# Two subtractions on the next pair's x, ordered behind a unit's last product on VectorE

## The chip, the cores and the metric

One Trainium2 chip, one core of it. The metric is the device time of one execution in microseconds (us); lower is better. The time before is the median of three runs.

## What is computed

Attention for 8 batches of 8 heads (576 positions, head size 64, a mask by blocks of 64), then a bilinear layer on its output: two products with 512 x 1536 weights, multiplied element by element, and a third product back to 512. In the reference:

```python
scores = scale * np.matmul(q, k.transpose(0, 1, 3, 2))
scores = np.where(mask, scores, -1000000000.0)
attn = np.exp(scores - np.max(scores, axis=-1, keepdims=True))
attn = attn / (np.sum(attn, axis=-1, keepdims=True) + 1e-09)
x = (attn @ v).transpose(0, 2, 1, 3).reshape(B * S, H * D)   # 4608 x 512
a, b = x @ w_a, x @ w_b                                      # 4608 x 1536 each
return (a * b) @ w_out                                       # 4608 x 512
```

## The kernel before

The kernel works with float32 values split in a high part that TensorE multiplies exactly (`fp32r`) and a low part, the remainder; a product is then three matmuls, high by high, high by low and low by high. ScalarE makes the high part with a cast (L110, L662 to L666), VectorE or GpSimd the low part with a subtraction (L113, L669 to L673).

Up to about 720 us attention and the first four of twelve blocks of the hidden size run together. The rest is the stage of the change: two passes (`ps_` 0 and 1) over six pairs (`tt` 0 to 5) of 384-column halves of x. A pair is worked on in **four units** (`pair_unit`, hidden blocks f = 4 to 7 in the first pass, 8 to 11 in the second) and then in **`pair_out`**, 96 matmuls into eight output tiles `pso`. In names such as `u_z_2_7` the first number is the pair and the second the block; the fourth unit of a pair has f = 7 or 11.

A unit forms seven products instead of eight (a Strassen-like scheme, which is why sums of x and of weights are needed). TensorE makes four products y, x, w, v; then three more are added on top of x, w and v in PSUM, each of which must wait until VectorE has read the sum that stands there: L708 (`u = x + u`) comes before the second product into x, L710 before that into w, L712 before that into v. L714 to L718 give the two results of the unit; the last, L718, is recorded as `last["hf"]`. ScalarE (L110) and GpSimd (L113) split each result in `h` tiles, high and low, which `pair_out` reads. `pair_out` starts with the first two output tiles over three units (18 matmuls) and then needs the `h` tiles of the fourth unit with index 1, high and low.

For the next pair `sums_x` makes the seven sums of x, once for each half of the 512 channels (`kp` 0 and 1). For each half it has four subtractions on VectorE (L659, L660, L661, L664; the first two need only the loaded x), four casts on ScalarE into `xh` (L662, L663 and L666 need the subtractions, L665 needs only the loaded x), and the remainders `xl`: for `kp` 0 all on VectorE, for `kp` 1 the first two on VectorE (L669, L670) and two on GpSimd (L672, L673). `xh` has three buffers and `xl` two, so a cast for `kp` 1 waits until TensorE has read the present pair's `xh` of `kp` 0 for the last time, near the end of the fourth unit. The loaded x, `xr`, has four buffers; a load waits until the remainders of the pair before are done. Loads and stores of this stage go through SyncE's queue in order.

`sums_x` is called in two steps: for `kp` 0 after the third unit (i = 2), for `kp` 1 after the fourth. The calls only write the instructions down. Where they end up on each engine is decided by a scheduler, which orders them by its own estimates and by dependences. `behind_of(ins, "hf")` adds an order without a semaphore: `ins` stands on its engine behind the instruction recorded last under that key. In the first pass up to pair 4 VectorE also converts weights for the second pass in the background (L139 to L178); these steps are already paced with `behind_of`.

Every engine runs its instructions in the order in which they stand.

Of the kernel before, what the change touches and what calls it, by code (L numbers as in the profile page):

```python
# [14 lines left out]
ALU = mybir.AluOpType  # L15
# [37 lines left out]
def attention_then_bilinear_ffn(  # L53
# [51 lines left out]
    def f32(ap):  # L105
        return ap.bitcast(F32)
# [10 lines left out]
    def behind_of(ins, key):  # L117
        if key in last:
            tc.add_manual_dep(ins.ins, last[key].ins.name, NOSYNC, reason="after work that is waited for")
# [533 lines left out]
    def sums_x(raw, kp, nm):  # L653

        hi = xk.tile([P, NW, T2], F32R, tag="xh", name=f"xh_{nm}_{kp}", bufs=3)
        t = tpool.tile([P, 3, T2], F32, tag="xt", name=f"xt_{nm}_{kp}")
        a, b = raw[2 * kp:2 * kp + 2]
        v = nc.vector
        v.tensor_tensor(t[:, 1], b[:, 1], a[:, 1], op=ALU.subtract)  # L659
        v.tensor_tensor(a[:, 1], a[:, 1], a[:, 0], op=ALU.subtract)  # L660
        v.tensor_tensor(t[:, 0], b[:, 1], a[:, 1], op=ALU.subtract)  # L661
        nc.scalar.copy(hi[:, 0:2], a)  # L662
        nc.scalar.copy(hi[:, 2:4], t[:, :2])  # L663
        v.tensor_tensor(t[:, 2], b[:, 0], t[:, 0], op=ALU.subtract)  # L664
        nc.scalar.copy(hi[:, 4:6], b)  # L665
        nc.scalar.copy(hi[:, 6], t[:, 2])  # L666
        yield
        lo = xk.tile([P, NW, T2], F32R, tag="xl", name=f"xl_{nm}_{kp}", bufs=2)
        v.tensor_tensor(lo[:, 0:2], a, f32(hi[:, 0:2]), op=ALU.subtract)  # L669
        v.tensor_tensor(lo[:, 2:4], t[:, :2], f32(hi[:, 2:4]), op=ALU.subtract)  # L670
        e = nc.gpsimd if kp else v
        e.tensor_tensor(lo[:, 4:6], b, f32(hi[:, 4:6]), op=ALU.subtract)  # L672
        e.tensor_tensor(lo[:, 6], t[:, 2], f32(hi[:, 6]), op=ALU.subtract)  # L673
        yield hi, lo
# [96 lines left out]
    for kp in range(KP):  # L771
        g = sums_x(raw, kp, "0_0")
        next(g)
        xs.append(next(g))
# [7 lines left out]
    for ps_ in range(2):  # L782
        fs = list(range(F1 + ps_ * F2, F1 + (ps_ + 1) * F2))
        for tt in range(NT2):
# [18 lines left out]
            nm = f"z{ps_}_{tt}"  # L803
            for i, f in enumerate(fs):
                if ps_ == 0 and tt == 0:
                    background(PER_F * (i + 1))
                for _ in pair_unit(f, xs, f"{nm}_{f}", hs, i == 0):
                    k += 1
                    background(start + k * T2 / 2.4 / pace)
                if i == 0 and not lastp:  # L810
                    raw = load_x((tt + 1) % NT2)
                if i == 1:
                    for x in todo[:6]:
                        load_part(*x)
                if i == 2 and not lastp:
                    nxt = [sums_x(raw, kp, f"{ps_}_{tt + 1}") for kp in range(KP)]
                    next(nxt[0])
                if ps_ == 0 and tt == NT2 - 1:
                    new_w(f + F2)
                    for kp in range(KP):  # L820
                        nc.sync.dma_start(
                            f32(w_sb[f + F2][0][:, kp]).rearrange("p j c n -> p (j c n)"), wabd[f - F1, kp])
# [53 lines left out]
```

## Time and profile before

| what | value |
| --- | --- |
| median of 3 runs (lowest, highest) | 1304.1 us (1302.88, 1304.73) |
| the profiled execution: its time, its span | 1307.22 us, 1305.4 us |
| TensorE busy | 1254.8 us, 96% of the span |
| VectorE, ScalarE, GpSimd busy | 997.9, 679.3, 546.4 us |
| mean granted TensorE clock | 0.984 |

In the profile PE is TensorE, PEld its weight loads, DVE VectorE, ACT ScalarE, POOL GpSimd and SP SyncE. Busy time is the union of an engine's instructions; "idle before" is the engine's pause ahead of an instruction, with what ended it. The profiled execution took 3.1 us more than the median of the plain runs.

### The profile page before, as it was taken

How to read it: one execution, taken by the hardware profiler on the slowest of the kernel's cores; microseconds unless marked ns; L12 is line 12 of the kernel's file. 1: busy time of each engine (PE TensorE's matmuls, PEld its weight loads, DVE VectorE, ACT ScalarE, POOL GpSimd, SP SyncE). 2: the span in 40 equal slices, each digit the busy share in tenths (PEclk: the TensorE clock that was granted, in tenths of full speed). 3: DMA queues.
4: the chain of work that ended last, by engine and by line, in shares of the span. 5: the costliest groups of instructions: out<-in, count | busy, mean ns of one | idle time of the engine just before them, and what ended most of it. 6: DMA issues, size and time to landing. Idle time of an engine off the chain costs nothing.

```text
span 1305.4 us, 23282 instructions
## 1 busy us (share of the span) xinstructions
PE 1254.8 (96%) x7849; PEld 1179.0 (90%) x7849; DVE 997.9 (76%) x2325; ACT 679.3 (52%) x1722; POOL 546.4 (42%) x681
## 2 busy tenths in 40 slices
PE   9998999999999999999998998999999899999998
PEld 5678888989999899898998998998999899999998
DVE  6878777777777777777789999899986476577563
ACT  5787777777777777777745433233332122222210
POOL 4676565555555555545521323124123124123131
PEclk8999999999999999999998999999999899999999
DMA  5557756667667676676234353563556541342231
GB/s 192 147 152 209 190 145 174 175 165 176 162 161 185 155 178 159 153 176 163 62 122 140 126 191 126 169 212 126 196 164 247 186 137 55 101 145 79 68 97 61
DMA packets 93495, 196.57 MB, mean 151 GB/s; under 512 B 11968, under 2 KB 52928, under 8 KB 93376
## 3 DMA queue, kind: packets, MB, share of 16 engines
q1 hardware_dynamic: 88768, 185.64, 50.3%
q10 hardware_dynamic: 4608, 9.44, 1.9%
q8 instruction: 63, 1.03, 0.3%
q14 instruction: 56, 0.46, 0.1%
HBM read 96.47 MB, written 47.19 MB: 110 GB/s over the span
## 4 chain that ended last, share of the span: by engine, by line
PE 58%; DVE 16%; DMA 11%; ACT 7%; issue 4%; SPq 1%; POOL 1%; ACTq 0%; DVEq 0%; POOLq 0%
PE pso_z L736 14%; PE ps L217 7%; PE psx_z L690 6%; PE psw_z L690 6%; PE psv_z L690 6%; PE tp L463 4%; DMA kp<-kT 4%; DMA k<-kp 4%; PE s L394 4%; PE psy_z L690 3%; PE av L507 2%; PE pso L217 2%; DMA q<-qp 2%; ACT ah L465 2%; DVE al L467 2%
## 5 line engine op out<-in xcount | busy, mean ns | idle before, releaser
L113 POOL TENSOR_TENSOR h_z<-u_z,h_z 128x384 fp32r<-128x384 f32 x96 | 113.6, 1184 | 399.3 <-ACT h_z L110 386.5
L217 PE MATMUL ps<-xh,wab 128*128 128x288 f32 x1024 | 240.6, 302 | 2.4 <-ACT a L241 2.4
L736 PE MATMUL pso_z<-h_z,wo 128*128 128x384 f32 x1152 | 207.1, 339 | 5.3 <-POOL h_z L113 5.3
L736 PEld LDWEIGHTS pso_z<-h_z,wo 128*128 128x128 f32 x1152 | 202.6, 190 | 7.8 <-POOL h_z L113 7.7
L467 DVE TENSOR_TENSOR al<-tp,ah 128x512 fp32r<-128x512 f32 x224 | 137.9, 617 | 65.0 <-ACT ah L465 61.6
L217 PEld LDWEIGHTS ps<-xh,wab 128*128 128x128 f32 x1024 | 172.6, 189 | 6.6 <-ACT a L241 2.7
L442 POOL TENSOR_SCALAR e<-e,rc 128x512 f32<-128x512 f32 (+3 forms) x256 | 153.2, 610 | 44.0 <-DVE rc L439 37.1
L217 PE MATMUL ps<-xl,wab 128*128 128x288 f32 x512 | 155.7, 304 | 0.0
L463 PE MATMUL tp<-ident,e 128*128 128x128 f32 x832 | 135.3, 277 | 10.6 <-DVE s L415 4.6
L465 ACT CAST ah<-tp 128x512 fp32r<-128x512 f32 x224 | 119.4, 535 | 44.6 <-PE tp L463 44.5
L110 ACT CAST h_z<-u_z 128x384 fp32r<-128x384 f32 x96 | 49.4, 514 | 165.0 <-DVE u_z L715 160.4
L690 PE MATMUL psx_z<-xh,wab 128*128 128x384 f32 x384 | 118.5, 344 | 7.7 <-DVE u_z L708 7.3
L217 PE MATMUL pso<-hh,wo 128*128 128x288 f32 x512 | 120.5, 305 | 3.2 <-ACT hh L110 3.1
L463 PEld LDWEIGHTS tp<-ident,e 128*128 128x128 f32 x832 | 102.3, 142 | 22.3 <-issue 6.2
L690 PE MATMUL psw_z<-xh,wab 128*128 128x384 f32 x384 | 117.0, 341 | 0.9 <-DVE u_z L710 0.8
L690 PE MATMUL psv_z<-xh,wab 128*128 128x384 f32 x384 | 117.0, 340 | 0.5 <-DVE u_z L712 0.4
L400 DVE TENSOR_REDUCE nm<-s 128x1 f32<-128x192 f32 (+3 forms) x256 | 109.5, 430 | 2.9
L403 ACT ACTIVATE e<-s,nm 128x192 f32<-128x192 f32 (+2 forms) x192 | 101.6, 529 | 7.1 <-DVE nm L400 4.4
L113 POOL TENSOR_TENSOR v<-vr,v 128x320 fp32r<-128x320 f32 x56 | 49.9, 891 | 127.2 <-ACT v L110 98.0
L217 PEld LDWEIGHTS ps<-xl,wab 128*128 128x128 f32 x512 | 96.5, 188 | 3.8
L113 POOL TENSOR_TENSOR hl<-hf,hh 128x288 fp32r<-128x288 f32 x64 | 54.1, 845 | 103.1 <-ACT hh L110 99.2
L217 PEld LDWEIGHTS pso<-hh,wo 128*128 128x128 f32 x512 | 88.3, 194 | 5.2 <-ACT hh L110 3.9
(147 smaller groups left out, 3013.7 us busy)
## 6 DMA issues: line engine op xcount, KB each, us to landing
k<-kp SPq DMA_DIRECT2D x112, 288.0 KB, 4.0
xr<-xd SPq DMA_DIRECT2D x48, 384.0 KB, 3.5
pt<-part SPq DMA_DIRECT2D x96, 192.0 KB, 3.5
q<-qp SPq DMA_DIRECT2D x112, 160.0 KB, 2.7
raww<-wab SPq DMA_DIRECT2D x24, 512.0 KB, 3.9
qp<-qT SPq DMA_DIRECT2D x32, 320.0 KB, 3.1
vr<-vm SPq DMA_DIRECT2D x64, 160.0 KB, 3.1
kp<-kT SPq DMA_DIRECT2D x32, 288.0 KB, 3.5
```

What stands on the lines that cost most here:

```text
L110: nc.scalar.copy(hi, src)
L113: return lo_eng.tensor_tensor(lo, src, f32(hi), op=ALU.subtract)
L217: mm = nc.tensor.matmul(ps, w_, d_, start=(i == 0), stop=(i == n - 1))
L394: mark = nc.tensor.matmul(ps[:, :w], qm[:, q0[t]:q0[t] + P], kk[:, :w], start=(i == 0), stop=(i == len(ks) - 1))
L400: nc.vector.tensor_reduce(nm[:, t:t + 1], view, axis=AX.X, op=ALU.max, negate=True)
L403: nc.scalar.activation(out, view, AF.Exp, bias=bias, accum_out=sm[:, t, :1])
L442: nc.gpsimd.tensor_scalar(ev, ev, rc[:, t:t + 1], 1.0, op0=ALU.mult, op1=ALU.mult)
L463: mark = nc.tensor.transpose(tp[:, c], src, ident)
L465: nc.scalar.copy(ah[:, :m, cols], tp[:, :m])
L467: nc.vector.tensor_tensor(al[:, :m, cols], tp[:, :m], f32(ah[:, :m, cols]), op=ALU.subtract)
L690: nc.tensor.matmul(ps, wt[:, i, iw], j[:, ix], start=start and kp == 0 and i == 0 and j is xh, stop=kp == KP - 1 and i == 1, skip_group_ch ...
L736: nc.tensor.matmul(ps, wt[:, a, osl], b, start=i == 0, stop=i == 3 * len(fs) - 1)
```

## The change

The first two subtractions of `sums_x`, for both halves `kp`, get `behind_of(..., "hf")`, except for the very first pair (`0_0`). When `kp` 0 is written down, the last recorded product is that of the third unit; when `kp` 1 is, it is already that of the fourth.

```diff
         v = nc.vector
-        v.tensor_tensor(t[:, 1], b[:, 1], a[:, 1], op=ALU.subtract)
-        v.tensor_tensor(a[:, 1], a[:, 1], a[:, 0], op=ALU.subtract)
+        for ins in (v.tensor_tensor(t[:, 1], b[:, 1], a[:, 1], op=ALU.subtract),
+                    v.tensor_tensor(a[:, 1], a[:, 1], a[:, 0], op=ALU.subtract)):
+            if nm != "0_0":
+                behind_of(ins, "hf")
         v.tensor_tensor(t[:, 0], b[:, 1], a[:, 1], op=ALU.subtract)
```

The scheduler then places more than these two differently. From L661 on, lines have two more in their number after the change (L665 becomes L667, L672 becomes L674, L708 becomes L710, L736 becomes L738). In the lists below a row is one instruction: line, operation, written and read tiles, shape.

VectorE across the end of pair 5 of the first pass and the start of the second pass, before. `xt_1` and `xr_1` belong to the pair after the next one; `pt` rows add an output tile:

```order
L673 TENSOR_TENSOR xl_6_0_13253<-xt_6_0_13173,xh_6_0_13172 128x384
L669 TENSOR_TENSOR xl_6_1_13268<-xr_0_13020,xh_6_1_13258 128x768
L670 TENSOR_TENSOR xl_6_1_13268<-xt_6_1_13259,xh_6_1_13258 128x768
L795 TENSOR_TENSOR pt_0_5_0_13092<-pso_0_z_5_13273,pt_0_5_0_13092 128x384
L795 TENSOR_TENSOR pt_1_5_0_13094<-pso_1_z_5_13283,pt_1_5_0_13094 128x384
L795 TENSOR_TENSOR pt_2_5_0_13096<-pso_2_z_5_13307,pt_2_5_0_13096 128x384
L795 TENSOR_TENSOR pt_3_5_0_13098<-pso_3_z_5_13322,pt_3_5_0_13098 128x384
L795 TENSOR_TENSOR pt_0_5_0_13100<-pso_0_z_5_13337,pt_0_5_0_13100 128x384
L659 TENSOR_TENSOR xt_1_0_13621<-xr_1_13472,xr_1_13470 128x384
L660 TENSOR_TENSOR xr_1_13470<-xr_1_13470 128x384
```

and after the change:

```order
L675 TENSOR_TENSOR xl_6_0_13253<-xt_6_0_13173,xh_6_0_13172 128x384
L659 TENSOR_TENSOR xt_6_1_13259<-xr_0_13022,xr_0_13020 128x384
L797 TENSOR_TENSOR pt_0_5_0_13092<-pso_0_z_5_13273,pt_0_5_0_13092 128x384
L660 TENSOR_TENSOR xr_0_13020<-xr_0_13020 128x384
L797 TENSOR_TENSOR pt_1_5_0_13094<-pso_1_z_5_13283,pt_1_5_0_13094 128x384
L663 TENSOR_TENSOR xt_6_1_13259<-xr_0_13022,xr_0_13020 128x384
L671 TENSOR_TENSOR xl_6_1_13268<-xr_0_13020,xh_6_1_13258 128x768
L666 TENSOR_TENSOR xt_6_1_13259<-xr_0_13022,xt_6_1_13259 128x384
L672 TENSOR_TENSOR xl_6_1_13268<-xt_6_1_13259,xh_6_1_13258 128x768
L797 TENSOR_TENSOR pt_2_5_0_13096<-pso_2_z_5_13307,pt_2_5_0_13096 128x384
```

The subtractions for the pair after the next one have left this place; the next pair's `kp` 1 has moved into it. The same holds at the ends of the other pairs.

ScalarE at the end of the same pair, before (the `h_z_5_7_1` row is the cast that `pair_out` needs first):

```order
L110 CAST h_z_5_6_0_13135<-u_z_5_6_13139 128x384
L662 CAST xh_6_1_13258<-xr_0_13020 128x768
L663 CAST xh_6_1_13258<-xt_6_1_13259 128x768
L110 CAST h_z_5_7_1_13215<-u_z_5_7_13218 128x384
L665 CAST xh_6_1_13258<-xr_0_13022 128x768
```

and after:

```order
L110 CAST h_z_5_6_0_13135<-u_z_5_6_13139 128x384
L664 CAST xh_6_0_13172<-xr_0_13016 128x768
L665 CAST xh_6_0_13172<-xt_6_0_13173 128x768
L668 CAST xh_6_0_13172<-xt_6_0_13173 128x384
L667 CAST xh_6_1_13258<-xr_0_13022 128x768
L110 CAST h_z_5_7_1_13215<-u_z_5_7_13218 128x384
```

The cast of `xr` that GpSimd's remainder reads (L665, now L667) has become the first cast for `kp` 1 and stands ahead of the `h` cast.

GpSimd at the same place, before:

```order
L113 TENSOR_TENSOR h_z_5_6_0_13136<-u_z_5_6_13139,h_z_5_6_0_13135 128x384
L113 TENSOR_TENSOR h_z_5_7_1_13216<-u_z_5_7_13218,h_z_5_7_1_13215 128x384
L672 TENSOR_TENSOR xl_6_1_13268<-xr_0_13022,xh_6_1_13258 128x768
L673 TENSOR_TENSOR xl_6_1_13268<-xt_6_1_13259,xh_6_1_13258 128x384
L113 TENSOR_TENSOR h_z_5_7_0_13214<-u_z_5_7_13217,h_z_5_7_0_13213 128x384
```

and after:

```order
L113 TENSOR_TENSOR h_z_5_6_0_13136<-u_z_5_6_13139,h_z_5_6_0_13135 128x384
L674 TENSOR_TENSOR xl_6_1_13268<-xr_0_13022,xh_6_1_13258 128x768
L113 TENSOR_TENSOR h_z_5_7_1_13216<-u_z_5_7_13218,h_z_5_7_1_13215 128x384
L113 TENSOR_TENSOR h_z_5_7_0_13214<-u_z_5_7_13217,h_z_5_7_0_13213 128x384
L675 TENSOR_TENSOR xl_6_1_13268<-xt_6_1_13259,xh_6_1_13258 128x384
```

The remainder of 768 columns has moved ahead of the low part that `pair_out` needs first. This swap is new at the ends of pairs 2 to 5 of the first pass and 0 to 4 of the second; at the ends of pairs 0 and 1 of the first pass GpSimd has this order already before the change.

On TensorE the order changes only in the first pass, among the units of pair 0 and near the ends of pairs 0 to 4. At pairs 1 to 4, six or seven of `pair_out`'s first 18 matmuls move ahead of the fourth unit's last products (ahead of the second product into x: 3, 2, 4 and 6 of them); at pair 0, five that stood there move back behind the unit.

## The prediction

> **What bounds the kernel now.** I read the page's busy times first, then the busy times by stretch, then TensorE's waits in the stage of the pairs, then the single pauses in the timeline.
>
> ```profile
> PE 1254.8 (96%) x7849; PEld 1179.0 (90%) x7849; DVE 997.9 (76%) x2325; ACT 679.3 (52%) x1722; POOL 546.4 (42%) x681
> 850.00:900.00 50.00, 48.96 (x275) 47.16 (x275) 47.86 (x85) 17.36 (x31) 14.56 (x12) 1.00 0.53 177
> 1100.00:1150.00 50.00, 50.00 (x286) 49.67 (x285) 34.86 (x56) 13.90 (x25) 15.65 (x12) 1.00 0.34 103
> PE psx_z L690 <- DVE u_z L708: 7.3, 9, 3.9
> PE pso_z L736 <- POOL h_z L113: 5.3, 3, 2.5
> ```
>
> TensorE is the bound: 50.00 of 50 us in a stretch of the second pass, 48.96 in the first pass, where VectorE with 47.86 is nearly full. So only what makes TensorE pause counts, and there are two such things (total us, times, longest): the sum x + u from VectorE (L708), and the low part `h` from GpSimd (L113) at a pair's end. The larger pauses one by one:
>
> ```profile
> 757.13 1.32 PE L736 MATMUL pso_z<-h_z,wo 128*128 128x384 f32 x5 [2.44 <-POOL h_z L113]
> 799.97 0.44 PE L690 MATMUL psx_z<-xh,wab 128*128 128x384 f32 x1 [0.51 <-DVE u_z L708]
> 809.28 1.01 PE L736 MATMUL pso_z<-h_z,wo 128*128 128x384 f32 x2 [2.54 <-POOL h_z L113]
> 852.78 0.44 PE L690 MATMUL psx_z<-xh,wab 128*128 128x384 f32 x1 [0.35 <-DVE u_z L708]
> 901.66 0.45 PE L690 MATMUL psx_z<-xh,wab 128*128 128x384 f32 x1 [0.95 <-DVE u_z L708]
> 949.51 0.44 PE L690 MATMUL psx_z<-xh,wab 128*128 128x384 f32 x1 [0.28 <-DVE u_z L708]
> 956.61 1.68 PE L736 MATMUL pso_z<-h_z,wo 128*128 128x384 f32 x8 [0.36 <-POOL h_z L113]
> 1024.85 0.69 PE L690 MATMUL psx_z<-xh,wab 128*128 128x384 f32 x1 [3.89 <-DVE u_z L708]
> ```
>
> The L736 rows are the ends of pairs 0, 1 and 4 of the first pass; the first four L690 rows are the fourth units of pairs 1 to 4; the last is the first unit of the second pass. A pause also costs clock afterwards. In stretches of 3.4 us (the number after the ACT and POOL columns is the granted clock):
>
> ```profile
> 140.10:143.50 3.40, 1.89 (x11) 1.42 (x11) 3.24 (x12) 3.24 (x9) 2.55 (x4) 1.00 0.66 185
> 143.50:146.90 3.40, 2.41 (x17) 2.16 (x17) 2.82 (x9) 1.92 (x7) 3.40 (x5) 1.00 0.30 62
> 689.70:693.10 3.40, 1.61 (x10) 1.40 (x11) 3.33 (x6) 1.38 (x4) 0.91 (x1) 1.00 0.00 1
> 693.10:696.50 3.40, 3.40 (x16) 3.40 (x16) 3.06 (x8) 1.79 (x5) 1.14 (x1) 0.50 0.58 192
> 757.90:761.30 3.40, 3.40 (x13) 3.40 (x12) 3.40 (x4) 1.35 (x2) 1.59 (x2) 0.50 0.67 199
> 809.10:812.50 3.40, 3.22 (x10) 3.22 (x11) 3.40 (x3) 0.83 (x1) 3.11 (x3) 0.50 0.65 222
> 1024.20:1031.00 6.80, 6.15 (x19) 6.15 (x20) 2.83 (x6) 0.51 (x1) 0.07 (x1) 0.50 0.89 340
> ```
>
> A stretch with TensorE idle for 1.8 us (busy 1.61) is followed by half clock; one idle for 1.5 us (busy 1.89) is not. Half clock costs half of the busy time in it: 1.7 us after pair 0, 1.6 after pair 1, 3.1 after the pass boundary. By the Trainium skill (TensorE: Matmul & The Clock Gate, "Part 1: The HAM clock gate") the clock is halved after at least one idle window of about 3.4 us. The rows above disagree: 1.8 us were enough. Were the Trainium skill right to the letter, none of the 2 us pauses that I forecast below would cost clock, and the time would be that of the third rival.
>
> **The change part by part.** First, **the pass boundary**. The subtractions for the pair after the next one leave VectorE's queue here:
>
> ```profile
> 1015.34 0.56 DVE L659 TENSOR_TENSOR xt<-xr,xr 128x384 f32<-128x384 f32 x1 [3.63 <-DMA xr<-xd]
> 1022.00 0.56 DVE L659 TENSOR_TENSOR xt<-xr,xr 128x384 f32<-128x384 f32 x1 [3.04 <-DMA xr<-xd]
> 1024.25 0.55 DVE L708 TENSOR_TENSOR u_z<-psx_z,u_z 128x384 f32<-128x384 f32 x1
> ```
>
> VectorE stands for 3.63 and 3.04 us before loads of x that are needed only a pair later, and L708, for which TensorE waits, is queued behind. After the change L708 follows the `pt` additions directly. Its x has then had a whole pair to land, so the wait moves nowhere on VectorE. What is late next is ScalarE's copy of y, which stands behind the cast of that same x; that cast now waits alone. I count the whole pause and its clock as gone: -(3.9 + 3.1) = **-7.0 us**. Bounds: 0 if ScalarE's cast takes the wait over, -7.0 if nothing does; I take -7.0, since the load is issued no later than before (on SyncE's queue behind the first three `pt` stores before, behind two of them and two `pt` loads now) and the copy had time to spare.
>
> Second, **the pair ends**, the largest term. What the new order on ScalarE and GpSimd does is read from pair 1, where GpSimd has that order already, and from pair 5:
>
> ```profile
> 802.94 0.84 ACT L662 CAST xh<-xr 128x768 fp32r<-128x768 f32 x1
> 803.26 1.05 PE L736 MATMUL pso_z<-h_z,wo 128*128 128x384 f32 x5
> 804.41 0.83 ACT L665 CAST xh<-xr 128x768 fp32r<-128x768 f32 x1
> 805.37 2.18 POOL L672 TENSOR_TENSOR xl<-xr,xh 128x768 fp32r<-128x768 f32 x1 [6.47 <-ACT xh L665]
> 807.50 1.72 POOL L113 TENSOR_TENSOR h_z<-u_z,h_z 128x384 fp32r<-128x384 f32 x1
> ...
> 999.45 0.84 ACT L662 CAST xh<-xr 128x768 fp32r<-128x768 f32 x1 [4.88 <-PE psv_z L690]
> 999.78 16.94 PE L736 MATMUL pso_z<-h_z,wo 128*128 128x384 f32 x96
> 1001.58 1.45 POOL L113 TENSOR_TENSOR h_z<-u_z,h_z 128x384 fp32r<-128x384 f32 x1 [5.86 <-ACT h_z L110]
> 1002.99 2.57 POOL L672 TENSOR_TENSOR xl<-xr,xh 128x768 fp32r<-128x768 f32 x1
> 1003.08 13.32 PEld L736 LDWEIGHTS pso_z<-h_z,wo 128*128 128x128 f32 x77 [0.16 <-POOL h_z L113]
> ```
>
> At pair 5 `h` is done at 1003.03 and TensorE wants it at about 1002.9: no slack at all. At pair 1 the remainder (2.18) runs first and TensorE waits 2.54 us. There the cast L665 was ScalarE's third, at 804.41; now it is the first and takes the place of L662 at 802.94, 1.47 us earlier. So the new pause is 2.54 - 1.47 = 1.07 us, at each end that has GpSimd's new order and an unchanged order on TensorE: pair 5 and pairs 0 to 4 of the second pass, six ends, **+6.4 us**. Bounds: GpSimd's `h` takes only 1.02 where VectorE leaves it alone,
>
> ```profile
> 993.34 1.02 POOL L113 TENSOR_TENSOR h_z<-u_z,h_z 128x384 fp32r<-128x384 f32 x1 [5.04 <-ACT h_z L110]
> ```
>
> and twice that, 2.04, would be the remainder's low end; then the pause is 0.2 us. With 2.57 for the remainder it is 1.5. I take 1.07, because VectorE runs the same L670, L718 and L672 beside it as at pair 1.
>
> At the ends of pairs 1 to 4 six or seven of the 18 matmuls that cover the wait now run ahead of the fourth unit's end. A matmul is 16.94 / 96 = 0.176 us, so six are 1.06 and the pause is 2.13 (2.3 at pair 4). Against before: pairs 2 and 3 +2.1 each, pair 4 2.3 - 0.36 = +1.9, pair 1 2.13 - 2.54 = -0.4. At pair 0 the cast is not freed so early, since it stands behind the `kp` 0 casts whose subtractions now run during the fourth unit; I take half of 1.47 and a little more for the shorter queue, -1.0 (bounds -1.8 and -0.5). Together **+4.7 us**.
>
> Third, **VectorE ahead of the second product into x**. In pairs 1 to 4 the fourth unit's L708 already arrives late (0.51, 0.35, 0.95, 0.28 above), and three of the moved subtractions now stand before it, four at pair 4; at pair 1 one weight step, L147, moves behind in exchange.
>
> ```profile
> L664 DVE TENSOR_TENSOR xt<-xr,xt 128x384 f32<-128x384 f32 x22 | 13.0, 590 | 0.3
> L660 DVE TENSOR_TENSOR xr<-xr 128x384 f32<-128x384 f32 x22 | 12.5, 568 | 0.2
> L661 DVE TENSOR_TENSOR xt<-xr,xr 128x384 f32<-128x384 f32 x22 | 12.1, 549 | 0.1
> L659 DVE TENSOR_TENSOR xt<-xr,xr 128x384 f32<-128x384 f32 x21 | 11.9, 566 | 6.7 <-DMA xr<-xd 6.7
> L147 DVE SCALAR_TENSOR_TENSOR sw<-raww,sw 128x512 int32<-128x512 int32 x12 | 11.8, 981 | 0.0
> ```
>
> Three are 1.68 us, four 2.27. The `pair_out` matmuls that moved ahead of the product fill 3, 2, 4 and 6 times 0.176. Net: pair 1, 1.68 - 0.98 - 0.53 = +0.2; pair 2, 1.68 - 0.35 = +1.3; pair 3, 1.68 - 0.70 = +1.0; pair 4, 2.27 - 1.06 = +1.2; **+3.7 us**. Where VectorE isn't full (pair 5 and the second pass) the two subtractions ahead of L708 fall into a pause of VectorE and cost nothing; without that pause they would cost 1.1 us a pair. The same four for `kp` 1 now run in the 16.9 us of `pair_out`, beside TensorE; the next unit needs their results after it. The removed work of the pair after the next one there only frees time that VectorE spends waiting.
>
> Fourth, **the clock**. The two drops after pairs 0 and 1 (1.7 + 1.6) are measured; whether they recur is an accident of where a stretch begins. Five pauses of about 2 us (pairs 0 to 4), of which by length about six in ten lie with 1.7 us or more in one stretch: 5 x 0.6 x 1.7 = 5.1, and 0.6 for the product waits of pairs 2 to 4, which become 1.5 to 1.9 us: **+2.4 us** net, between -3.3 (none) and +6.9 (all).
>
> Loads: SyncE's queue has the loads of `xr` for `kp` 1 later, behind the first four `pt` stores, because their buffers come free later. They are read a pair later. GpSimd issues no DMA here.
>
> **The sum**: -7.0 + 6.4 + 4.7 + 3.7 + 2.4 = +10.2 us. Against the profiled execution that is a span of 1305.4 + 10.2 = 1315.6; its whole time, 1307.2, lies 3.1 above the median of the runs, so I put the sum on the median: 1304.1 + 10.2 = 1314.
>
> **The rivals.** *Faster: GpSimd ends early.* Everything hangs on 2.18 + 1.72 us of GpSimd. With 2.04 + 1.02, six ends cost 0.2 (1.3 in all), pairs 2 to 4 give 1.3 + 1.3 + 1.1, pairs 0 and 1 -1.8 - 1.3, no new pause is long enough for half clock (-3.3): with +3.7 and -7.0 the sum is about -4, 1300 us. For it: the 1.02 of 993.34. Against: 1.45 to 1.72 at the pair ends. It decides once the two take about 0.6 us less than at pair 1. 10%; another 10% for the ground between, within 0.2% (2.6 us, about what a measurement of this kernel tells from no change).
>
> *The pass boundary keeps its wait.* The copy of y stands on ScalarE behind the cast that waits for the load; if the load lands 3 us later than before, the pause returns: +17 us, 1321. Against it speaks the order on SyncE's queue. 7%.
>
> *No clock is lost on the new pauses.* If each of the five is split between two stretches, or 2 us prove too short after all, the clock term is -3.3 in place of +2.4: +4.5, 1308.6. The row with 1.8 us idle speaks against the second way, nothing against the first. 13%. The Trainium skill's rule on the clock, named above, would give this time too.
>
> My forecast keeps 60%. Slower 0.80, same 0.10, faster 0.10. The 8-in-10 range leaves out the fast rival and the highest ends of the terms: 1303 to 1322; the likeliest case alone is 1310 to 1319.
>
> **What would show it.** In the trace after: no wait of L659 for `xr` and no 3.9 us pause at the start of the second pass; a pause of about 1.1 us before `pso_z` on GpSimd's `h` at the ends of pair 5 and of five pairs of the second pass, about 2 at pairs 1 to 4, with the remainder ahead of `h` on GpSimd and starting some 0.6 us after the unit's end; waits for L708 of 1.5 to 1.9 us in the fourth units of pairs 2 to 4. The total for TensorE waiting on GpSimd rises from 5.3 to about 17 us. Wrong I would be if GpSimd's two instructions take 3 us or less together, or if a new wait at the pass boundary takes the old one's place.

## The result, and the profile after

The changed kernel is slower. Its median is 1311.83 us over seven runs (1308.57 to 1317.35), against 1304.1 us for seven runs of the kernel before on the same chip (1297.71 to 1304.73): ratio 1.0078, 95% interval 1.0049 to 1.0106. The ratio is that of the means, 1312.84 and 1302.71, which differ by 10.1 us; the medians differ by 7.7. The forecast was 1314 in 1303 to 1322. The profiled execution took 1311.74 us, with a span of 1309.7.

The instructions of the first 715 us are the same in both kernels, and the time to the stage of the pairs differed by 5.9 us between the two profiled executions, in favour of the changed kernel. What the change does is therefore read from the stage alone, from the start of its first `psy` matmul to the end of TensorE's last one: 582.55 us before, 592.20 after, **+9.65 us**. The same measure pair by pair, each from its first `psy` to the next pair's first (us; the last pair of the second pass takes 46.48 in every kernel):

| | pair 0 | 1 | 2 | 3 | 4 | 5 | second pass 0 | 1 to 4, each | stage |
| --- | --- | --- | --- | --- | --- | --- | --- | --- | --- |
| before | 52.12 | 52.79 | 48.61 | 48.81 | 48.43 | 46.46 | 52.97 | 46.46 to 46.47 | 582.55 |
| after | 48.78 | 52.40 | 51.85 | 53.45 | 52.45 | 47.77 | 47.83 | 47.77 to 47.83 | 592.20 |

So pairs 0 to 4 of the first pass lost 8.2 us together, pair 5 and the five pairs of the second pass that have a successor lost 1.3 each, and the first pair of the second pass, where the 3.89 us wait was, gained 6.5 beside that loss.

TensorE's waits in the stage of the changed kernel (total us, times, longest) answer to the rows of 7.3 and 5.3 before:

```profile
PE pso_z L738 <- POOL h_z L113: 15.9, 11, 2.1
PE psx_z L692 <- DVE u_z L710: 5.5, 6, 1.7
```

The wait for GpSimd's `h` has tripled and now comes at all eleven pair ends. The total of the wait for x + u fell only because the 3.89 us at the start of the second pass are gone. The single pauses in the timeline (start us, busy us, then the pause in brackets): first the pair ends (of the six equal ones, from pair 5 on, the first and the last), then the fourth units of pairs 1 to 4.

```profile
748.78 0.45 PE L738 MATMUL pso_z<-h_z,wo 128*128 128x384 f32 x1 [1.65 <-POOL h_z L113]
799.60 0.45 PE L738 MATMUL pso_z<-h_z,wo 128*128 128x384 f32 x1 [1.80 <-POOL h_z L113]
853.05 0.45 PE L738 MATMUL pso_z<-h_z,wo 128*128 128x384 f32 x1 [2.09 <-POOL h_z L113]
904.90 0.44 PE L738 MATMUL pso_z<-h_z,wo 128*128 128x384 f32 x1 [2.08 <-POOL h_z L113]
957.38 0.69 PE L738 MATMUL pso_z<-h_z,wo 128*128 128x384 f32 x1 [1.97 <-POOL h_z L113]
1006.71 0.44 PE L738 MATMUL pso_z<-h_z,wo 128*128 128x384 f32 x1 [1.05 <-POOL h_z L113]
...
1245.73 0.45 PE L738 MATMUL pso_z<-h_z,wo 128*128 128x384 f32 x1 [1.04 <-POOL h_z L113]
```

```profile
791.59 0.44 PE L692 MATMUL psx_z<-xh,wab 128*128 128x384 f32 x1 [0.80 <-DVE u_z L710]
844.59 0.44 PE L692 MATMUL psx_z<-xh,wab 128*128 128x384 f32 x1 [1.38 <-DVE u_z L710]
896.78 0.45 PE L692 MATMUL psx_z<-xh,wab 128*128 128x384 f32 x1 [1.71 <-DVE u_z L710]
949.70 0.44 PE L692 MATMUL psx_z<-xh,wab 128*128 128x384 f32 x1 [1.11 <-DVE u_z L710]
```

One pair end of the second pass, where nothing else is tight: the unit's last matmul starts at 1049.86 and `pair_out` at 1050.03. GpSimd's remainder (L674) takes its queue at 1050.67, `h` follows and ends at 1054.48, and TensorE goes on at 1054.53.

```profile
1050.67 2.12 POOL L674 TENSOR_TENSOR xl<-xr,xh 128x768 fp32r<-128x768 f32 x1 [4.86 <-ACT xh L667]
1052.76 1.72 POOL L113 TENSOR_TENSOR h_z<-u_z,h_z 128x384 fp32r<-128x384 f32 x1
1054.53 3.76 PE L738 MATMUL pso_z<-h_z,wo 128*128 128x384 f32 x20 [1.04 <-POOL h_z L113]
```

At the start of the second pass VectorE's queue now holds only `pt` additions ahead of L710, and L710 waits for ScalarE's copy of y alone; TensorE has no pause there.

```profile
1020.39 0.56 DVE L797 TENSOR_TENSOR pt<-pso_z,pt 128x384 f32<-128x384 f32 x1 [1.53 <-PE pso_z L738]
1023.11 0.56 DVE L710 TENSOR_TENSOR u_z<-psx_z,u_z 128x384 f32<-128x384 f32 x1 [2.16 <-ACT u_z L709]
```

The granted clock (last column but two) in stretches of 3.4 us around the ends of pairs 1, 2 and 4; the second column is TensorE's busy time:

```profile
797.00:800.40 3.40, 1.60 (x9) 1.28 (x8) 3.40 (x4) 0.51 (x1) 3.18 (x3) 0.99 0.19 25
800.40:803.80 3.40, 3.40 (x13) 3.40 (x12) 3.40 (x5) 0.00 (x0) 0.84 (x1) 0.50 0.47 125
...
851.60:855.00 3.40, 1.95 (x11) 1.95 (x12) 3.40 (x4) 0.51 (x1) 2.88 (x2) 1.00 0.13 30
855.00:858.40 3.40, 3.40 (x22) 3.40 (x21) 3.40 (x8) 1.76 (x3) 0.00 (x0) 1.00 0.66 223
...
954.00:957.40 3.40, 1.43 (x10) 1.11 (x8) 3.40 (x4) 0.73 (x2) 3.33 (x2) 1.00 0.39 154
957.40:960.80 3.40, 3.40 (x11) 3.40 (x12) 3.40 (x5) 0.07 (x1) 1.47 (x1) 0.50 0.41 116
```

Half clock followed the ends of pairs 1, 3 and 4. The 2.09 us pause of pair 2 was split between two stretches, 1.45 of it in the second, and cost no clock.

### The profile page after: what moved, and what is told of

It reads as the page before. It is cut to its first block, busy times and chain, and to the rows that moved or that the text cites. A ratio compares the mean times of both kernels' runs of the same rounds, so it can differ in the third digit from the quotient of the medians.

```text
span 1309.7 us, 23283 instructions
## 1 busy us (share of the span) xinstructions
PE 1252.8 (96%) x7849; PEld 1177.1 (90%) x7849; DVE 991.4 (76%) x2325; ACT 681.5 (52%) x1722; POOL 538.7 (41%) x681
## 4 chain that ended last, share of the span: by engine, by line
PE 63%; DVE 16%; DMA 7%; ACT 6%; issue 3%; POOL 3%; SPq 1%; ACTq 0%; POOLq 0%; DVEq 0%
PE pso_z L738 13%; PE ps L217 9%; PE psx_z L692 6%; PE psw_z L692 6%; PE tp L463 5%; PE psv_z L692 5%; PE s L394 4%; PE pso L217 3%; PE av L507 3%; PE psy_z L692 3%; DMA kp<-kT 2%; DMA k<-kp 2%; DMA q<-qp 2%; POOL xl L674 2%; PE sl L394 2%
## 5 line engine op out<-in xcount | busy, mean ns | idle before, releaser
L738 PE MATMUL pso_z<-h_z,wo 128*128 128x384 f32 x1152 | 211.1, 341 | 15.9 <-POOL h_z L113 15.9
L738 PEld LDWEIGHTS pso_z<-h_z,wo 128*128 128x128 f32 x1152 | 204.5, 192 | 19.4 <-POOL h_z L113 19.4
```

The costliest lines, as they stand in the source:

```text
L738: nc.tensor.matmul(ps, wt[:, a, osl], b, start=i == 0, stop=i == 3 * len(fs) - 1)
```

## The experiments

**The theory** (A): time is lost where GpSimd's remainder stands ahead of `h`, in the half clock that the longer pauses bring, and in the subtractions ahead of x + u; time is won at the start of the second pass, where VectorE no longer waits for loads. **The rivals**: GpSimd would be late beside VectorE's remainders in any order (B); the wait at the start of the second pass comes back elsewhere (D); and VectorE is full anyway, so what stands ahead of x + u does not matter. All stages (us) come from the one profiled execution of each kernel, all ratios from the runs, each against the kernel before on its own chip:

| run | stage | ratio to before, 95% interval |
| --- | --- | --- |
| before | 582.55 | 1 |
| the change | 592.20 | 1.0078, 1.0049 to 1.0106 |
| change, GpSimd's `h` first | 574.66 | 0.9948, 0.9930 to 0.9965 |
| before, GpSimd's `h` first | 576.37 | 0.9955, 0.9938 to 0.9973 |
| behind the first unit, `h` first | 570.60 | 0.9918, 0.9895 to 0.9941 |
| change for one pair | 576.02 | 0.9963, 0.9943 to 0.9984 |
| change for `kp` 0 alone | 588.22 | 1.0080, 1.0052 to 1.0108 |
| change for `kp` 1 alone | 583.22 | 1.0037, 1.0016 to 1.0059 |
| remainder twice | 628.85 | 1.0388, 1.0344 to 1.0431 |
| remainder one and a half times | 614.79 | 1.0305, 1.0262 to 1.0348 |
| `kp` 1 alone, `h` first | 567.44 | 0.9920, 0.9894 to 0.9945 |

In all ten rows the stage gives a larger gain or a smaller loss than the ratio (for `kp` 1 alone +0.7 us of stage against +0.37% of 1300, which is 4.8 us). So the 582.55 of the kernel before may be some us above its usual stage. That is not shown: its profiled execution was 3.1 us above its median, but it also came to the stage latest of all eleven, at 719.34 us against 708.8 to 718.2. Comparisons between two changed kernels don't hang on it.

Each stage is one execution, so a difference of about 1 us between two of them says little. An example: in pair 0's first unit TensorE waits 0.60 to 1.05 us for x + u in the kernel before and in seven of the runs, and not at all in the changed kernel, with `kp` 0 alone and in the run of the last row. Yet TensorE, VectorE and ScalarE have the same order throughout in the changed kernel, in the run with `h` first (1.05) and in the two with a longer remainder (0.91 and 0.78).

**GpSimd's `h` first, in the changed kernel.** One more order on GpSimd: the remainder of `kp` 1 behind the fourth unit's first low part.

```diff
-        e.tensor_tensor(lo[:, 4:6], b, f32(hi[:, 4:6]), op=ALU.subtract)
+        r = e.tensor_tensor(lo[:, 4:6], b, f32(hi[:, 4:6]), op=ALU.subtract)
+        if kp and nm != "0_0":
+            behind_of(r, "hb")
...
-        split(hb, lb, t, nc.scalar, nc.gpsimd)
+        last["hb"] = split(hb, lb, t, nc.scalar, nc.gpsimd)
```

> The changed kernel, with GpSimd's remainder of 768 columns ordered behind the low part h that pair_out needs first, at all eleven pair ends. Everything else stands as in the changed kernel. Theory A (the time was lost because the remainder stood ahead of h): the pauses for h, 15.9 us in all, fall to about 2.5: none at pair 0, pair 5 and the second pass, where h would end about 3.1 us after the unit's end and TensorE wants it at 3.2, and 0.4 to 0.8 at pairs 1 to 4, where 6 or 7 of the 18 covering matmuls run ahead. No half clock is left after a pair end (three drops of about 1.7 go). Together about -18 us against the changed kernel: 1294, ratio to the kernel before about 0.992. Rival B (GpSimd is simply slow beside VectorE's remainders, which now stand at the same place, so h is late in whatever order): h takes 1.5 to 1.7 us but starts late, pauses stay at 1 us and more, and the ratio stays above 1.003.

In the traces TensorE, VectorE and ScalarE run the same instructions in the same order as in the changed kernel; only GpSimd's order differs. The stage fell by 17.5 us to 574.66, the median is 1293.86, the ratio 0.9948. TensorE's waits, and one pair end of the second pass, where `pair_out` starts at 1039.99 and runs through:

```profile
PE psx_z L694 <- DVE u_z L712: 6.5, 7, 1.7
PE pso_z L740 <- POOL h_z L113: 3.1, 5, 0.9
```

```profile
1039.99 6.19 PE L740 MATMUL pso_z<-h_z,wo 128*128 128x384 f32 x34
1041.72 1.52 POOL L113 TENSOR_TENSOR h_z<-u_z,h_z 128x384 fp32r<-128x384 f32 x1 [5.94 <-ACT h_z L110]
1043.20 2.58 POOL L674 TENSOR_TENSOR xl<-xr,xh 128x768 fp32r<-128x768 f32 x1
```

`h` ends 3.25 us after the unit, just in time, though it takes 1.52 beside VectorE as theory A allowed. The pauses for `h` fell from 15.9 to 3.1 us (0.4 to 0.9 at pairs 0 to 4), and the clock shows no half stretch between 712 and 1292 us. Rival B falls: the order alone made the pauses. The waits for x + u in the fourth units stayed (0.77, 1.41, 1.70, 1.01).

**GpSimd's `h` first, in the kernel before.** The same edit without the change.

> The kernel before, with the same order on GpSimd: only the ends of pairs 0 and 1 of the first pass change, the only two where the remainder stood ahead of h. Theory A: the pauses of 2.44 and 2.54 us go (to 0 to 0.3) and with them the two drops to half clock behind them (1.7 and 1.6), so about -8 us: 1296, ratio 0.994. The 3.89 us pause at the start of the second pass stays. Rival B: the two pauses stay above 1.5 us, ratio above 0.997. Rival C (the clock drops are not due to these pauses): only the pauses go, -5 us, 0.996, and half clock still shows near 758 and 809 us.

Stage 576.37 (-6.2), ratio 0.9955. The pauses of 2.44 and 2.54 us went, to 0.48 and nothing, and so did both half clock stretches, which rules C out. But only pair 0 kept its gain (52.12 to 48.95); pair 1 won 1.9 instead of 4.2, since a new wait had come up in its first unit:

```profile
764.02 0.44 PE L692 MATMUL psx_z<-xh,wab 128*128 128x384 f32 x1 [1.84 <-DVE u_z L710]
...
762.35 0.56 DVE L661 TENSOR_TENSOR xt<-xr,xr 128x384 f32<-128x384 f32 x1
762.95 0.56 DVE L664 TENSOR_TENSOR xt<-xr,xt 128x384 f32<-128x384 f32 x1
763.42 0.55 DVE L710 TENSOR_TENSOR u_z<-psx_z,u_z 128x384 f32<-128x384 f32 x1
```

VectorE is full there without a break; the pause at pair 0's end had let it catch up with the subtractions for the pair after the next one, which stand ahead of L710. The change, which moves just those subtractions away, has no such wait in pair 1's first unit.

**One pair alone.** `if nm == "1_1":` in place of `if nm != "0_0":`, so that the order is given for one pair only, whose subtractions (two for each half) stood at the start of the second pass.

> The change for one pair alone: the second pair of the second pass, the pair whose subtractions made VectorE wait for loads at the start of the second pass. All else stands as in the kernel before, but at the end of the second pass's first pair GpSimd's remainder now stands ahead of h. Theory A: the pause of 3.89 us at the start of the second pass goes and 3.1 us of half clock with it; one new pause of 1.05 us, worth 1.2: -5.8 us, 1298, ratio 0.9955. Rival D (the wait comes back elsewhere, on ScalarE's copy of y behind the cast, or one pair later): the pause shows at another place, and the ratio is 0.998 to 1.002.

Stage 576.02 (-6.5), ratio 0.9963, median 1295.73. The first pair of the second pass takes 47.80 us in place of 52.97, with the one new pause that was expected at its end:

```profile
1048.43 0.44 PE L738 MATMUL pso_z<-h_z,wo 128*128 128x384 f32 x1 [1.05 <-POOL h_z L113]
```

No wait came up elsewhere; rival D falls. Of the 6.5 us only 5.2 belong to this place. The rest is pair 1 of the first pass (51.23 in place of 52.79), whose 2.56 us pause happened to cost no clock in this execution.

**The first half alone, the second half alone.** The condition with `and kp == 0`, or with `and kp == 1`.

> The order of the change for the first half (kp 0) alone. At the ends of pairs 0 to 4 of the first pass everything stands as after the change (remainder ahead of h on GpSimd, matmuls of pair_out ahead of the fourth unit's end, subtractions ahead of x + u); at pair 5 and in the second pass h is ahead of the remainder as before. The start of the second pass has no subtractions of a later pair. Theory A: the six ends that took 47.8 us instead of 46.5 in the changed kernel go back to 46.5, all else stays: stage of the pairs 592.2 - 6 x 1.3 = 584.3 against 582.6 before and 592.2 after the change; ratio about 1.001. Rival (the second half's order makes the whole loss): 576, ratio 0.994.

> The order of the change for the second half (kp 1) alone. GpSimd has the remainder ahead of h at all eleven ends, ScalarE its cast ahead of the h cast, but VectorE's subtractions for kp 0 and TensorE's order stay as before. Theory A: a pause of about 1.05 us (1.3 us of pair time) at pairs 2 to 5 and at the five ends of the second pass; at pair 1 about 1.05 in place of 2.54, and its half clock gone; the pause at the start of the second pass gone (6.5). Stage: 582.6 - 6.5 - 5 (pairs 0 and 1) + 9 x 1.3 - 0.4 = 582.4, ratio 1.000; the waits for x + u in the fourth units of pairs 1 to 4 stay at 0.3 to 0.9 us. Rival (the pauses at the ends come from the subtractions of kp 0 on VectorE, by the casts that they delay): no pause of 1 us at the nine ends, 571, ratio 0.99.

The second half did as theory A said: stage 583.22 (582.4 expected), pauses of 1.01 to 1.05 us at pairs 2, 3, 5 and the five ends of the second pass, and the waits for x + u back at 3.2 us in all. Pair 4 went otherwise than expected, with two waits (0.51 and 1.20) and a half clock behind them. The rival of this run (no pauses of 1 us at these ends, 571) falls. The first half missed by 3.9 us, and its ratio is 1.0080 where 1.001 was expected; the rival there (576, 0.994) lies further off. Pairs 0 to 4 took 1.5 us less than after the change, since half clock came twice and not three times. But pair 5 and the five pairs of the second pass took 47.4, not 46.5. One of them:

```profile
1042.35 1.62 DVE L659 TENSOR_TENSOR xt<-xr,xr 128x384 f32<-128x384 f32 x2
1043.90 1.38 DVE L660 TENSOR_TENSOR xr<-xr 128x384 f32<-128x384 f32 x1
1045.80 0.45 PE L692 MATMUL psx_z<-xh,wab 128*128 128x384 f32 x1 [0.31 <-DVE u_z L710]
1052.74 0.44 PE L738 MATMUL pso_z<-h_z,wo 128*128 128x384 f32 x1 [0.26 <-POOL h_z L113]
```

Three subtractions stood ahead of x + u there (L659 for both halves), and beside GpSimd's low part the three took 2.9 us, so that even with VectorE's slack TensorE waited 0.31; two more than in the changed kernel (L660, L663) stood ahead of L716, on which `h` depends, and `h` came 0.26 late. With 0.16 for each pause that the idle time leaves out (below) that is 0.9 a pair. I had counted only GpSimd's order there and not what else the scheduler had moved on VectorE.

**Behind the first unit.** Both halves' subtractions behind the product of the present pair's first unit, two units earlier than in the change for `kp` 0 and three for `kp` 1, with GpSimd's `h` first.

```diff
-                behind_of(ins, "hf")
+                behind_of(ins, "h0")
...
+                if i == 0:
+                    last["h0"] = last["hf"]
```

> The subtractions of both halves are ordered behind the present pair's first unit's product, two units earlier than in the change, and GpSimd's remainder behind h as in the run above. VectorE then has no subtraction of the next pair at the start of the second pass, and almost none ahead of the sum x + u of the fourth units. Theory A: no pause at the start of the second pass (-7 us), no pause above 0.5 us for h, waits of 0.3 to 0.9 us for x + u in the fourth units as before the change: about 4 us below the first run of this set, 1290, ratio 0.989. Rival (the subtractions ahead of x + u cost nothing beside what VectorE has to do anyway, since it is full in the first pass): the same time as the first run of this set, within 1.5 us.

Stage 570.60, 4.1 below the run that it was to be compared with, median 1289.17, ratio 0.9918.

```profile
PE psx_z L694 <- DVE u_z L712: 2.9, 4, 1.1
PE pso_z L740 <- POOL h_z L113: 1.9, 4, 0.6
```

The wait for x + u fell from 6.5 to 2.9: what stands ahead of it does matter. The single waits were not where I had put them, though: none is left in the fourth units of pairs 1 to 4, and the longest, 1.12, stands in pair 4's third.

**The second half alone, with GpSimd's `h` first.** This differs from the first experiment in the order of `kp` 0 alone.

> The order of the change for the second half (kp 1) alone, with GpSimd's remainder behind h. Against the run with the changed kernel and GpSimd's order (stage 574.7 us) only the first half's subtractions differ: they stand where the scheduler puts them, not ahead of x + u in the fourth units, and TensorE's order is that of before. Theory A (the first half's subtractions on VectorE delay x + u in pairs 1 to 4 and take cover from the pair ends): waits for x + u in those units 0.5, 0.3, 0.3 and 0.9 us in place of 0.77, 1.41, 1.70 and 1.01, pauses for h under 0.4 us, none at the start of the second pass, no half clock: stage about 569, ratio about 0.990. Rival (VectorE is full there in any order, and the wait moves elsewhere): 573 to 575, ratio 0.994.

Stage 567.44, the shortest of all (569 expected), median 1289.47, ratio 0.9920.

```profile
PE psx_z L694 <- DVE u_z L712: 3.1, 7, 1.0
...
PE pso_z L740 <- POOL h_z L113: 1.0, 2, 0.7
```

The stages differ by 7.2 us (574.66 - 567.44). Of that, 1.1 lies in pair 0, where this execution happens to lack the wait in the first unit. The order of the first half costs the other 6: the waits for x + u and the cover that TensorE's matmuls lose at pairs 1 to 4, and 0.15 in each of the six pairs after them that have a successor. This version and the one behind the first unit beat both kernels; their ratios don't tell them apart.

**The remainder twice, and one and a half times.** In the changed kernel GpSimd computes the remainder a second time, whole or its first 384 columns; the result is the same.

```diff
         e.tensor_tensor(lo[:, 4:6], b, f32(hi[:, 4:6]), op=ALU.subtract)
+        if kp and nm != "0_0":
+            e.tensor_tensor(lo[:, 4:6], b, f32(hi[:, 4:6]), op=ALU.subtract)
```

> The changed kernel, with GpSimd's remainder of 768 columns computed twice in a row (same result). At nine ends (pairs 0, 2, 3, 5 and the second pass) both stand ahead of h, at pairs 1 and 4 one. Theory A: those nine pauses grow by one remainder of 1.9 to 2.1 us, from 1.05 to 3.1 in the second pass and from 1.7 to 2.1 to about 3.9 in the first: +18 us. Theory on the clock (about 1.8 us idle in one 3.4 us stretch suffice): nearly each of the nine is followed by half clock, worth 1.7, against two of them in the changed kernel: +11. Stage about 621. If half clock needed a stretch without any matmul, it would follow two or three of them only: about 611. Rival B (GpSimd's order does not set the pauses): under 600.

> As the run above, but only 384 of the 768 columns a second time. At the same nine ends the pause grows by 1.0 to 1.1 us: to 2.1 in the second pass and at pair 5, about 3 at pairs 0, 2 and 3: +9.5 us. Clock: a pause of 2.1 us lies with 1.7 or more in one 3.4 us stretch in six cases of ten, so half clock after 3 or 4 of the six ends and after all three long ones, with pairs 1 and 4 as in the changed kernel: 8 drops against 3, +8.5. Stage about 610. If two microseconds were too short for half clock in general: 602. Rival B: under 597.

Stages 628.85 (621 expected) and 614.79 (610). With the whole remainder twice the pauses of the second pass became 3.5 us, not 3.1:

```profile
1067.66 2.12 POOL L674 TENSOR_TENSOR xl<-xr,xh 128x768 fp32r<-128x768 f32 x1 [4.85 <-ACT xh L667]
1069.86 2.41 POOL L676 TENSOR_TENSOR xl<-xr,xh 128x768 fp32r<-128x768 f32 x1
1073.99 0.69 PE L740 MATMUL pso_z<-h_z,wo 128*128 128x384 f32 x1 [3.51 <-POOL h_z L113]
```

The second copy took 2.41 beside VectorE. The pauses for `h` came to 38.3 us in all, 22.4 more than in the changed kernel where 18 were forecast. Half clock followed all nine doubled ends, three of them for two stretches. With half of it added the pauses were 2.71 to 2.74 in the second pass (2.1 expected), and half clock came eight times, at all three long ends of the first pass and at five of the six others. That is as many as forecast, but not in the places named: three or four of the six others and pairs 1 and 4, where none came. Both confirm that the length of GpSimd's queue ahead of `h` sets the pause; how much 384 columns cost there I had put too low, at 1.0 to 1.1, where the pause grew by 1.67.

## Why the prediction was right

Term by term, by its own steps:

- **The pass boundary**, -7.0 forecast. Measured on the pair that has it: 52.97 before, 46.46 in the run behind the first unit, which has neither the wait nor the new end: -6.5. VectorE does not wait there any more, and ScalarE's copy came in time. The forecast's 7.0 is nearly what TensorE had lost when the half clock ended: against the next pair, which has no pause, it was 4.05 us behind at the first matmul after the wait and 6.90 behind 19 matmuls later. It then made up 0.4, since its matmuls started 0.173 us apart for the rest of the four units where the next pair's start 0.177 apart; why is open.
- **Six pair ends**, +6.4 forecast with 1.07 each. The pause is 1.04 to 1.05 at each of the six, so the step from pair 1 (2.54 - 1.47) held within 0.03 us. But a pair grew by 1.30 to 1.37, and the six together by 8.0. With `kp` 1 alone, which has the same pauses, a pair grew by 1.16 to 1.21: some 0.15 more than the idle time, which the sum left out. The remaining 0.1 to 0.2 belongs to the two subtractions of `kp` 0 ahead of x + u, which the prediction put at nothing here; in the run with `h` first, which has them without the pauses, these pairs took 46.6 us, where pairs without a pause had taken 46.46 before the change.
- **The ends of pairs 0 to 4**, +4.7 forecast. Pauses of 1.65, 1.80, 2.09, 2.08 and 1.97 against 2.44, 2.54, none, none and 0.36 give +4.3. The half that I took at pair 0 was nearly right (1.44 forecast); pairs 1 and 4 came 0.3 below.
- **VectorE ahead of the second product into x**, +3.7 forecast. The waits were 0.80, 1.38, 1.71 and 1.11, against 0.51, 0.35, 0.95 and 0.28 before: +2.9. Pairs 2 and 4 lie below the 1.5 to 1.9 that I named. By experiment the order of `kp` 0 costs about 6 us with GpSimd's order mended, more than these waits, since the matmuls that run ahead in this wait are missing as cover at the pair's end; in the forecast that part stood under the pair ends.
- **The clock**, +2.4 forecast net of the two drops in the first pass of before. Three drops came after pauses of 1.80, 2.08 and 1.97, against two before. A drop costs about 1.6, not 1.7: pairs that differ in little but one drop differ by 1.56 to 1.59 (pair 1 before and with one pair alone, pairs 1 and 3 in the changed kernel and with `kp` 0 alone). So the term is +1.6. How many drops come is in part luck, as it was with two there and three here. The Trainium skill (TensorE: Matmul & The Clock Gate, "Part 1: The HAM clock gate") asks for an idle stretch of about 3.4 us; the runs again disagree, since no pause in the changed kernel's stage was longer than 2.1. By that rule the time would have been the 1308.6 of the third rival.

The sum of these measured terms is -6.5 + 8.0 + 4.3 + 2.9 + 1.6 = +10.3 against +9.65 for the stage; the forecast's was +10.2. The difference of 0.6 is the wait in pair 0's first unit, which the profiled execution of the kernel before had (0.60) and that of the changed kernel happened to lack. So the mechanism was right in its main steps, but the forecast owes part of its closeness to terms that err in both directions: the six pair ends too small by 1.6, three others too large by 0.4 to 0.8, the boundary's gain 0.5 too large.

Of the rivals, GpSimd did not end early (2.12 and 1.72 us at the ends), the wait at the pass boundary did not come back, and the clock was lost. Their mechanisms were the right ones to weigh: the experiment with `h` first shows what the first would have been worth.

## What to carry to other kernels

An order that only moves two subtractions on one engine can swap instructions on three others, so after such an edit compare the queue of the engine that delivers last, here GpSimd, at each place where the bound engine waits. When a helper engine holds both an urgent and a patient instruction, order the patient one behind explicitly: here that one order turned a loss of 0.8% into a gain of 0.5%. Leaving out the half of the change that loads the full engine added about 0.3% more by the ratios, whose intervals overlap, and 6 us by the stages. A pause that lets a full engine catch up is not all gain when it goes: when the pause at the end of pair 0 went, a wait of 1.84 us came up in the first unit of pair 1.

## What the runs showed of the hardware

**VectorE and GpSimd take turns.** At the end shown above, the VectorE instruction beside GpSimd's two is this one:

```profile
1051.45 2.16 DVE L672 TENSOR_TENSOR xl<-xt,xh 128x768 fp32r<-128x768 f32 x1
```

GpSimd's remainder ends at 1052.79, this one 0.82 later at 1053.61, GpSimd's `h` 0.87 after that at 1054.48. The same VectorE shape took 0.95 alone (1054.16 in the kernel before, L670), `h` 1.02. So each ends nearly its plain time after the other's end, as if it had stood until then. The Trainium skill (SBUF — State Buffer, "Who interferes with whom") says that a VectorE instruction with two inputs in SBUF and a GpSimd instruction that reads SBUF exclude each other, in the order of their start; the trace agrees. It makes the price of an instruction on GpSimd depend on what VectorE started just before: 384 columns cost 1.67 us of pause, not 1.0.

**A pause costs more than its idle time.** The six pauses of 1.05 us show 1.38 us from one matmul's start to the next, where 0.177 is usual: 1.20 lost, 0.16 more than the idle time. The idle time is counted from the modelled end of the matmul before, which the profile draws 0.34 us long though the next one usually starts after 0.177.

**Half clock has no sharp threshold in these records.** Take stretches of 3.413 us on the grid that the drops themselves show. In the stage of the pairs, over these runs, the least idle time that was followed by half clock was 1.72 us, while 1.84 (3.4 - 1.56) and 1.90 us (3.4 - 1.50) went without:

```profile
947.80:951.20 3.40, 1.68 (x8) 1.10 (x7) 3.40 (x5) 1.02 (x2) 2.14 (x3) 1.00 0.27 97
951.20:954.60 3.40, 3.40 (x12) 3.39 (x12) 3.40 (x7) 0.54 (x1) 1.01 (x1) 0.50 0.49 135
```

```profile
804.20:807.60 3.40, 1.56 (x9) 1.24 (x8) 3.40 (x4) 1.42 (x4) 3.19 (x2) 1.00 0.43 113
807.60:811.00 3.40, 2.68 (x15) 2.68 (x16) 3.40 (x3) 0.84 (x1) 3.40 (x3) 1.00 0.71 233
```

```profile
1116.80:1120.20 3.40, 1.50 (x9) 1.50 (x10) 3.40 (x3) 0.31 (x1) 3.14 (x3) 1.00 0.39 97
1120.20:1123.60 3.40, 3.40 (x21) 3.40 (x21) 3.40 (x8) 2.19 (x3) 0.00 (x0) 1.00 0.37 135
```

The first is the run with `kp` 1 alone (two pauses, 0.51 and 1.20, in one stretch), the second the one pair alone, the third the remainder one and a half times. From 50 us on in all eleven traces, half clock always followed a stretch at full clock with more than 2.0 us idle, and the least that it followed was 1.64 (at 176.9 us in the run behind the first unit). Ahead of 50 us it came after far less (0.3 us at 42.6 in the changed kernel), which was not followed up. A stretch that was itself at half clock was followed by a second one with 0.6 us idle (752.6 to 759.4 with the remainder twice), and ahead of the stage with 0.25 (705.9 with `kp` 0 alone). Since the ends of matmuls are modelled, the edge may lie in the records.
